# Halving the width of the output projection's matmuls in a fused attention and feed-forward kernel

## The chip, the cores and the metric

The kernel runs on one core of a Trainium2 chip. A core has a matrix engine (TensorE, "PE" in the profile, whose weight loads are listed apart as "PEld"), a vector engine (VectorE, "DVE"), a scalar engine (ScalarE, "ACT"), a general engine (GpSimd, "POOL") and a queue engine (SyncE, "SP"), and 16 DMA engines. Matmuls read SBUF and write PSUM. The metric is the device time in microseconds; lower is better.

A matmul has a stationary operand (up to 128 x 128, put into the array by a weight load) and a moving operand (128 rows, up to 512 columns, streamed through it). The result has as many columns as the moving operand.

## The reference

For each of 8 batches, with u and v of 3008 x 256 and z of 3008 x 64, and then for all 24064 rows together:

```
scores = (z @ z.T) / 3008
attn   = max(scores, 0) ** 2
x      = u * (attn @ v)              # 24064 x 256
h      = x @ w_in                    # 256 -> 2048
g      = h * cos(h)
out    = g @ w_out                   # 2048 -> 256, float32
```

The last product is what the change concerns; the text calls it y.

## The kernel before, in words

Rows are worked on in slots of 512: six per batch, the last of 448, so NSLOT = 48 slots. The feed-forward part has 48 blocks too: those with index 5 modulo 12 have 384 rows (`mwidth`), and the 64 rows that they leave over are put into the last block of the next batch (tile xodd), so that all others have 512. Operands are 16-bit floats, sums are fp32 in PSUM.

A slot has two phases. Phase A (`phase_a`) computes attention: score matmuls (line 187, two 64-row matmuls at a time), ReLU on ACT (line 200), the square on DVE (lines 205 and 208), and value matmuls with v as stationary operand (line 254), summed in the PSUM tiles M and E. DVE and ACT join the two partial sums (lines 266, 267) and multiply by u (line 282), which gives x, with the model width on partitions.

Phase B (`phase_b`) computes the feed-forward part in an order that is written out by hand:

```
seq_b = "h0 y0 h1 y1 h2 y2 h3 y3 h4 y4 h5 y5 y6 y7 st h6 h7".split()
```

An h step (`emit_h`, line 396) makes 256 of the 2048 inner columns: four matmuls of 512 columns into an E tile, with w_in blocks as stationary operand, then cos by a sine on ACT (line 404) and h * cos(h) on DVE (line 406) into a tile g with the inner width on partitions. A y step (`emit_y`, line 426) takes one such g tile of two inner blocks `ft`: for each, and for each of the up to four 128-row blocks `k`, `y_block` issues one matmul (line 418) whose stationary operand is the 128 x 128 block of g and whose moving operand is the 256 columns of w_out16 for that ft. The sums of the four row blocks lie in the two M banks, two per bank (`y_bank`), over all 16 ft; the first matmul of a bank starts its sum, the last stops it. The step `st` (`store_y`) copies M to SBUF on ACT (line 437) and sends it out from SP's queue (line 448). The steps h0 to h3 of the order above belong to the same block as its y steps, and are the block's last four; h4 to h7 are the first four of the next block, whose y steps come one phase B later. There are 47 phases B. The last block goes through `last_y`, which does the row blocks 0 and 1 beside the last h steps and then 2 and 3 one after the other, block 3 in an E bank.

At the start, z of the first batch is turned on the PE: `turn_on_pe` (line 517) issues 24 matmuls in transpose mode, each with a new 128 x 128 block of z as stationary operand and 128 columns of an identity as moving operand. Some matmuls on a tile of zeros (lines 532 and 556) stand around them.

The program order on each engine is the order in which the kernel text emits (`manual_schedule`); nothing moves instructions between engines or in time. Transposes of attention pieces (line 240) and of u (line 156), and stores, go through SP's queue; loads go through POOL's.

Of the kernel before, what the change touches and what calls it, by code (L numbers as in the profile page):

```python
# [14 lines left out]
def kernel(  # L15
# [9 lines left out]
    nc = tc.nc  # L25
# [6 lines left out]
    P = 128  # L32
# [5 lines left out]
    NFT = Dff // P  # L38
# [26 lines left out]
    w_out16 = kpool.tile([P, NFT, D], FP16, name="w_out16")  # L65
# [38 lines left out]
    z16s, zTs, vs, u16s, uTs, xs, gs = {}, {}, {}, {}, {}, {}, {}  # L104
# [281 lines left out]
    def mwidth(m):  # L386
        return 3 * P if m % (2 * NC) == NC - 1 else CW
# [23 lines left out]
    def y_bank(m, k):  # L411
        if m == NSLOT - 1 and k == 3:
            return E[0][:, 0, 0:D]
        return M[k // 2][:, (k % 2) * D:(k % 2 + 1) * D]

    def y_block(m, ft, k):
        final = m == NSLOT - 1
        nc.tensor.matmul(  # L418
            y_bank(m, k),
            gs[m, ft // 2][:, ft % 2, k * P:(k + 1) * P],  # L420
            w_out16[:, ft, :],
            start=(ft == 0 and (k % 2 == 0 or (final and k == 3))),
            stop=(ft == NFT - 1 and (k % 2 == 1 or k == mwidth(m) // P - 1 or (final and k == 2))),
        )

    def emit_y(m, i):
        for ft in range(2 * i, 2 * i + 2):
            for k in range(mwidth(m) // P):
                y_block(m, ft, k)

    def store_y(m):
        nblk = mwidth(m) // P
# [19 lines left out]
    def last_y(m):  # L452
        b, J = m // NC, m % NC
        for i in range(4):
            emit_h(m, 4 + i)
            for ft in range(2 * i, 2 * i + 2):
                y_block(m, ft, 0)
                y_block(m, ft, 1)
        for ft in range(8, NFT):
            y_block(m, ft, 0)  # L460
            y_block(m, ft, 1)
        for k in range(4):
            if k >= 2:
                for ft in range(NFT):
                    y_block(m, ft, k)
            o = opool.tile([P, 2, D], FP32, name="o")
            nc.scalar.activation(
                o[:, 0, :], y_bank(m, k),
                AF.Copy, bias=0.0, scale=inv_s2,
            )  # L470
            t0 = b * S + J * CW + k * P
            if k < 3:
                nc.sync.dma_start(out[t0:t0 + P, :], o[:, 0, :])
            else:
                nc.sync.dma_start(out[t0:t0 + H, :], o[0:H, 0, :])
                nc.scalar.dma_start(out[b * S - H:b * S, :], o[H:P, 0, :])
# [3 lines left out]
    def phase_b(s):  # L480
        for c in seq_b:
            i = int(c[1]) if c[1].isdigit() else 0
            if c == "st":
                store_y(s - 2)
            elif c[0] == "y":
                emit_y(s - 2, i)
            elif i < 4:
                emit_h(s - 2, 4 + i)
            elif s - 1 < NSLOT:
                emit_h(s - 1, i - 4)  # L490
            if c in ("h1", "h3", "h5"):
                emit_turns((0, 0), 1)
# [154 lines left out]
```

## Time and profile before

| | |
|---|---|
| median of 8 runs | 1231.68 us (1228.88 to 1235.65) |
| profiled execution | 1229.59 us |
| its span, first to last instruction | 1227.8 us |
| mean granted PE clock | 0.999 of full speed |
| PE busy | 99%, 9775 matmuls and 9775 weight loads |
| DVE busy / ACT busy | 65% / 66% |
| y matmuls (line 418) | 3008, mean 273 ns from start to modelled end |
| y weight loads (line 418) | 3008, mean 98 ns |

The profile comes from one execution. Matmuls are pipelined: one starts before the former has ended, so the mean duration of one is longer than the distance between starts, and only the latter adds up along the PE. In the tables of groups, the first number after the bar is the time in which at least one instruction of the group was busy, then comes the mean of one; after the second bar stands how long the engine sat idle just before them, and what ended that. In rows in order of time, the first number is the start, the second is how long the stretch lasted, both in microseconds, and "xN" is the number of instructions.

### The profile page before, as it was taken

Reading aid. Unit: us, or ns where it says so; the run is one execution under the profiler, and the core shown is the slowest. Engines: PE = TensorE matmul, PEld = TensorE weight load, DVE = VectorE, ACT = ScalarE, POOL = GpSimd, SP = SyncE. Lnnn points to the kernel's source line nnn. Section 1 sums busy time; section 2 is a strip of 40 time slices with the busy share of each in tenths; the row PEclk is TensorE's granted clock in tenths of the full one; section 3 lists DMA queues with packets and bytes.
Section 4 is the critical chain, followed back from the end, with each engine's and each line's share of the span. In section 5 each row is a group of like instructions: output and inputs, shape, how many; then the busy total and the mean of one; then the engine's idle time right before and its main releaser. Section 6 shows DMA issues by size and latency. Waiting matters only on the chain.

```text
span 1227.8 us, 23274 instructions
## 1 busy us (share of the span) xinstructions
PE 1217.6 (99%) x9775; PEld 694.9 (57%) x9775; DVE 803.0 (65%) x943; ACT 810.4 (66%) x923; POOL 131.3 (11%) x184
## 2 busy tenths in 40 slices
PE   8999999999999999999999999999999999999998
PEld 4455555555555556555555555655555555555565
DVE  6856666666666666666666666666666666666555
ACT  7856666667666666667666676666666666666445
POOL 3120300003000030000310002100211001000000
PEclk9999999999999999999999999999999999999999
DMA  9998998349773499725977359763697637953201
GB/s 155 182 172 153 138 158 142 63 98 165 140 126 74 89 153 165 120 70 100 172 129 123 71 102 165 145 125 65 115 178 123 114 73 106 157 103 70 47 18 52
DMA packets 467162, 144.80 MB, mean 118 GB/s; under 512 B 391537, under 2 KB 466801, under 8 KB 467057
## 3 DMA queue, kind: packets, MB, share of 16 engines
q1 hardware_dynamic: 368304, 110.11, 50.2%
q0 software_dynamic: 97216, 32.78, 28.3%
q8 instruction: 76, 1.25, 0.4%
q10 hardware_dynamic: 1536, 0.43, 0.2%
q14 instruction: 30, 0.24, 0.1%
HBM read 66.32 MB, written 24.64 MB: 74 GB/s over the span
## 4 chain that ended last, share of the span: by engine, by line
PE 94%; DMA 2%; issue 2%; ACT 1%; DVE 1%; POOL 0%; ACTq 0%; DVEq 0%; POOLq 0%
PE M L418 26%; PE E L396 26%; PE M L254 19%; PE E L254 18%; PE E L187 5%; DMA u<-in_u_dram 1%; ACT r L200 1%; DMA uT<-u 1%; PE E L532 0%; DVE g L406 0%; ACT c L404 0%; DVE A L208 0%; DVE s L267 0%; PE E L418 0%; DVE A L205 0%
## 5 line engine op out<-in xcount | busy, mean ns | idle before, releaser
L406 DVE SCALAR_TENSOR_TENSOR g<-E,c 128x1024 f16<-128x1024 f32 (+1 forms) x384 | 456.3, 1201 | 218.2 <-ACT c L404 217.0
L404 ACT ACTIVATE c<-E 128x1024 f16<-128x1024 f32 (+1 forms) x384 | 380.9, 1006 | 183.0 <-PE E L396 182.6
L200 ACT ACTIVATE r<-E 128x512 f16<-128x512 f32 (+1 forms) x342 | 327.9, 967 | 112.2 <-PE E L187 106.9
L418 PE MATMUL M<-w_out,g 128*128 128x256 f16 x2992 | 373.7, 273 | 1.0 <-DVE g L406 0.6
L254 PEld LDWEIGHTS <-v 64*128 64x128 f16 x4512 | 217.7, 94 | 259.7 <-issue 19.8
L396 PE MATMUL E<-x,w_in 128*128 128x512 f16 (+1 forms) x1408 | 347.4, 374 | 1.4 <-DVE g L406 0.7
L418 PEld LDWEIGHTS <-g 128*128 128x128 f16 x3008 | 294.2, 98 | 94.0 <-DVE g L406 0.9
L254 PE MATMUL M<-A,v 64*128 64x512 f16 (+1 forms) x2256 | 282.6, 372 | 0.3 <-DVE s L267 0.3
L254 PE MATMUL E<-A,v 64*128 64x512 f16 (+1 forms) x2256 | 277.5, 372 | 0.0
L205 DVE TENSOR_TENSOR A<-r 128x1024 f16<-128x1024 f16 x240 | 165.5, 692 | 103.9 <-ACT r L200 102.9
L396 PEld LDWEIGHTS <-w_in 128*128 128x128 f16 x1536 | 146.4, 98 | 127.2 <-issue 21.7
L187 PE MATMUL E<-zT 64*128 64x512 f16 (+2 forms) x684 | 125.2, 361 | 2.3 <-DVE zT L527 1.1
L437 ACT ACTIVATE o<-M 128x512 f32<-128x512 f32 x94 | 50.2, 585 | 63.4 <-PE M L418 63.4
L136 POOL DMA_DIRECT2D u<-in_u_dram x48 | 36.8, 770 | 461.5 <-DMA uT<-u 460.5
L208 DVE TENSOR_TENSOR A<-r 128x512 f16<-128x512 f16 (+1 forms) x102 | 57.7, 567 | 41.6 <-ACT r L200 40.6
L136 POOL DMA_DIRECT2D v<-in_v_dram x48 | 35.9, 754 | 401.8 <-PE E L187 338.7
L282 DVE TENSOR_TENSOR x<-s,uT 128x512 f16<-128x512 f32 (+1 forms) x88 | 59.5, 679 | 8.3 <-DMA uT<-u 5.5
L187 PEld LDWEIGHTS <-zT 64*128 64x128 f16 x684 | 34.6, 94 | 43.1 <-issue 4.3
L267 DVE TENSOR_TENSOR s<-E,s 128x512 f32<-128x512 f32 (+1 forms) x48 | 32.6, 680 | 34.1 <-ACT s L266 34.1
L266 ACT COPY s<-E 128x512 f32<-128x512 f32 (+1 forms) x48 | 27.7, 578 | 39.7 <-PE E L254 39.7
L267 DVE TENSOR_TENSOR s<-M,s 128x512 f32<-128x512 f32 (+1 forms) x48 | 32.3, 674 | 6.0 <-ACT s L266 6.0
L266 ACT COPY s<-M 128x512 f32<-128x512 f32 (+1 forms) x48 | 27.5, 573 | 8.2 <-PE M L254 7.8
(34 smaller groups left out, 118.2 us busy)
## 6 DMA issues: line engine op xcount, KB each, us to landing
out_dram<-o SPq DMA_DIRECT2D x87, 256.0 KB, 2.6
v<-in_v_dram POOLq DMA_DIRECT2D x40, 256.0 KB, 6.8
u<-in_u_dram POOLq DMA_DIRECT2D x40, 256.0 KB, 9.1
z<-in_z_dram POOLq DMA_DIRECT2D x14, 368.0 KB, 15.1
A<-A SPq DMA_TRANSPOSE x207, 4.4
v<-in_v_dram POOLq DMA_DIRECT2D x8, 192.0 KB, 10.9
u<-in_u_dram POOLq DMA_DIRECT2D x8, 192.0 KB, 4.4
out_dram<-o SPq DMA_DIRECT2D x10, 128.0 KB, 2.7
```

The costliest lines, as they stand in the source:

```text
L136: nc.gpsimd.dma_start(t[:, 0:full, :], src[b, g * CW:g * CW + full * P, :].rearrange("(j p) d -> p j d", p=P),)
L187: nc.tensor.matmul(e[:, t, 0:W], zT[t * H:(t + 1) * H, k * P:(k + 1) * P], zT[t * H:(t + 1) * H, J * CW:J * CW + W], start=True, stop=True,)
L200: nc.scalar.activation(r[:, :, 0:W], e[:, :, 0:W], AF.Relu)
L205: nc.vector.tensor_tensor(a4, r4, r4, ALU.mult)
L208: nc.vector.tensor_tensor(a4, r[:, :, 0:W], r[:, :, 0:W], ALU.mult)
L254: nc.tensor.matmul(bank[:, 0:width(J)], vs[b, k // 4][t * H:(t + 1) * H, k % 4, dh * P:(dh + 1) * P], value_rhs(b, J, k, t), start=start, ...
L267: nc.vector.tensor_tensor(s1[:, 0:W], b1[:, 0:W], s0[:, 0:W], ALU.add)
L282: nc.vector.tensor_tensor(x[:, dh, 0:nk * P].rearrange("p (k j) -> p k j", j=P), s1[:, 0:nk * P].rearrange("p (k j) -> p k j", j=P), uT[:, ...
L396: nc.tensor.matmul(e[:, f, 0:W], w_in16[:, k, ft * P:(ft + 1) * P], x[:, k, 0:W], start=(k == 0), stop=(k == 1),)
L404: nc.scalar.activation(c[:, :, 0:W], e[:, :, 0:W], AF.Sin, bias=half_pi, scale=inv_s2)
L406: nc.vector.scalar_tensor_tensor(g[:, :, 0:W], e[:, :, 0:W], 1.0, c[:, :, 0:W], ALU.mult, ALU.mult)
L418: nc.tensor.matmul(y_bank(m, k), gs[m, ft // 2][:, ft % 2, k * P:(k + 1) * P], w_out16[:, ft, :], start=(ft == 0 and (k % 2 == 0 or (final ...
```

## The change

Each y matmul of 256 columns becomes two of 128 columns, one for each half `q` of the output width. In `emit_y` the half is a loop around the row blocks k, so that for each ft four matmuls with four different g blocks write the first half, and then four with the same four g blocks write the second; every matmul has a weight load of another block than the one before it. In `last_y`, which calls `y_block` without a half, the two halves of a row block follow each other. The start flag stands on half 0 of the first matmul of a bank, the stop flag on half 1 of the last.

```diff
-    def y_block(m, ft, k):
+    def y_block(m, ft, k, d=None):
         final = m == NSLOT - 1
-        nc.tensor.matmul(
-            y_bank(m, k),
-            gs[m, ft // 2][:, ft % 2, k * P:(k + 1) * P],
-            w_out16[:, ft, :],
-            start=(ft == 0 and (k % 2 == 0 or (final and k == 3))),
-            stop=(ft == NFT - 1 and (k % 2 == 1 or k == mwidth(m) // P - 1 or (final and k == 2))),
-        )
+        for q in range(2) if d is None else (d,):
+            nc.tensor.matmul(
+                y_bank(m, k)[:, q * P:(q + 1) * P],
+                gs[m, ft // 2][:, ft % 2, k * P:(k + 1) * P],
+                w_out16[:, ft, q * P:(q + 1) * P],
+                start=(ft == 0 and q == 0 and (k % 2 == 0 or (final and k == 3))),
+                stop=(ft == NFT - 1 and q == 1 and (k % 2 == 1 or k == mwidth(m) // P - 1 or (final and k == 2))),
+            )
 
     def emit_y(m, i):
         for ft in range(2 * i, 2 * i + 2):
-            for k in range(mwidth(m) // P):
-                y_block(m, ft, k)
+            for q in range(2):
+                for k in range(mwidth(m) // P):
+                    y_block(m, ft, k, q)
```

## The prediction

> **What bounds the kernel now.** I read the page's shares first, then the waits, then the chain, and last the order of time in one phase B and in the first microseconds.
>
> ```profile
> span 1227.8 us, 23274 instructions
> PE 1217.6 (99%) x9775; PEld 694.9 (57%) x9775; DVE 803.0 (65%) x943; ACT 810.4 (66%) x923; POOL 131.3 (11%) x184
> PE 94%; DMA 2%; issue 2%; ACT 1%; DVE 1%; POOL 0%; ACTq 0%; DVEq 0%; POOLq 0%
> ```
>
> PE is busy 99% of the span and carries 94% of the chain that ended last. A busy PE row alone proves little, because matmul records overlap and their ends are modelled. The idle columns decide:
>
> ```profile
> L418 PE MATMUL M<-w_out,g 128*128 128x256 f16 x2992 | 373.7, 273 | 1.0 <-DVE g L406 0.6 <-DVE s L267 0.4
> L396 PE MATMUL E<-x,w_in 128*128 128x512 f16 x1280 | 322.0, 379 | 1.4 <-DVE g L406 0.7 <-DVE s L267 0.7
> L418 PEld LDWEIGHTS <-g 128*128 128x128 f16 x3008 | 294.2, 98 | 94.0 <-DVE g L406 0.9 <-issue 0.6
> ```
>
> All y matmuls together (L418: 2992 into M, 16 into E) waited 1.0 us in the whole run, and those of h (L396) 1.4 us. So whatever one y matmul costs more is paid in full. The 273 ns of one is start to modelled end; what counts is the distance between starts, and that is read from the chain, where a stretch ends at the start of the next:
>
> ```profile
> 118.05 2.62 PE M L418 x24
> ```
>
> 24 matmuls in 2.62 us: 109.2 ns for one of 256 columns. In the same place, h of 512 columns takes 0.86 us for four (117.18 to 118.05), about 216 ns each. A halving of the columns from 512 to 256 thus saves not quite half: 2 x 109.2 - 216 = 2.4 ns are paid per matmul, however many columns it has.
>
> The changed kernel's new form, 128 columns with a fresh 128x128 stationary block every time, is already in this trace: the transposes of z at the start (L517; stationary z16, moving id16).
>
> ```profile
> 5.85 0.40 PE L517 MATMUL turned<-id,z 128*128 128x128 f16 x4
> 6.08 0.39 PE L517 MATMUL turned_e<-id,z 128*128 128x128 f16 x4
> 6.30 0.59 PE L556 MATMUL M<-warm 128*128 128x512 f16 x2
> 5.84 0.45 PEld L517 LDWEIGHTS <-z 128*128 128x128 f16 x8 [0.42 <-DVE zT L527]
> ```
>
> The first three rows are the matmuls, the fourth is the weight loads of the eight transposes. The second four take from 6.08 to 6.30: 0.22 us, 55 ns each. All eight, with the first that has no load ahead of it, take 0.45 us: 56 ns each. Eight loads fit into the same 0.45 us although each is listed with 98 ns, so loads overlap one another and a load is not a limit at 98 ns. These are transposes and write 16-bit results, where y accumulates in fp32; that they stream at the same rate is my assumption, supported by the 2.4 ns that both have above half of the next size.
>
> **What the Trainium skill says.** "TensorE: Matmul & The Clock Gate", section "Wait — 56ns, not 53.3ns?", gives start-to-start as N ÷ 2.4 GHz plus about 2.5 ns: 55.6 ns at 128 columns and 215.7 at 512. The trace agrees: 55 to 56, 109.2 and 216. The same page, section "Step-by-step: what each phase is for", says that the loads of the next block run while the present matmul streams, through a read port of their own; the eight overlapped loads agree. But its section "Back-to-back issue gap" gives, for a sustained stream of load and matmul pairs, about 81 ns at 128 columns and 131 at 512. The 512 figure is contradicted here (216), and no run of 128 columns longer than eight is in this trace, so 81 stays as a rival.
>
> **The change part by part.**
>
> Removed: 3008 matmuls of 256 columns with 3008 loads. On the path: 3008 x 109.2 ns = 328.5 us.
>
> Added: 6016 matmuls of 128 columns with 6016 loads. Columns streamed and products are the same. The price of one lies between 55 ns (second four transposes) and 56.3 ns (all eight, including the uncovered first). The rule from the halving, 109.2/2 + 1.2 = 55.8 ns, lies between them, and I take it. The cost is 2 x 55.8 - 109.2 = 2.4 ns per old matmul: 3008 x 2.4 = 7.2 us. With 55 ns it would be 0.8 x 3008 = 2.4 us, with 56.3 ns 3.4 x 3008 = 10.2 us. The low end needs a fixed cost that shrinks with the matmul, and the rounding of 0.22 us to 0.01 allows 54 to 56, so I lean up: 7.5 us.
>
> The second load of each g block: 3008 more loads, hidden behind the previous matmul, cost nothing while a load needs less than the 55.8 ns of that matmul. The eight transposes show that it fits. If that cover were gone and loads went at their listed 98 ns end to end, a pair would be 196 ns and the kernel 3008 x 87 = 261 us slower; the eight loads in 0.45 us exclude that.
>
> Moved: within one ft, emit_y now goes over the four k for columns 0 to 127 and then again for 128 to 255. The same accumulator address is hit again after 8 x 55.8 = 446 ns instead of 4 x 109.2 = 437; in last_y's one-k loops after 112 instead of 109. Nothing shorter, so no new hazard; I set zero. The M banks still alternate every two matmuls as k goes 0, 1, 2, 3. The last y of a block still closes both halves, so store_y's copy (L437) starts when the PE gets there; it had 63.4 us of waiting for L418 and is behind no one.
>
> Waits and DMAs: none is added. The first y of each g tile waits for DVE's g as before. Behind PE nothing is late that isn't late by the same 0.16 us per slot (7.5 us over 47 slots); ACT at 66% and DVE at 65% have room, so they follow. Instruction fetch: 19550 PE instructions become 25566. In a slot, 64 y matmuls and 32 of h take 7.0 + 6.9 = 13.9 us for 192 instructions, 72 ns each; afterwards 320 instructions in 14.1 us, 44 ns each, and 28 ns each inside a run of y. Phase A's pairs run two loads and two matmuls per 216 ns, 54 ns per instruction, the densest sustained rate that this trace shows. So the supply is shown for 54, and for 28 only in a burst of eight pairs that may have been queued up. Zero if the queue refills quickly; if 54 were its limit, 320 x 54 = 17.3 us per slot instead of 14.1, which is 3.2 x 47 = 150 us. I take zero: no idle time of PE is put down to issue in a dense stretch.
>
> Sum: +7.5 us on the profiled execution, 1229.59 us with its span of 1227.8, gives 1237.1 with a span of 1235.3. The profiled execution is 2.1 us under the median of the runs, 1231.68; against that the forecast is 1239.2.
>
> **The rivals.**
>
> (a) Sustained pairs don't keep up: either instruction supply at 54 ns (1231.7 + 150 = 1382) or the page's 81 ns per pair ((162 - 109.2) x 3008 = 159 us, 1391). For it: no long run of this form is in the trace, and the 24 matmuls of y5 to y7 in each slot become 48 on end. Against it: the eight transposes, and 24 y at a steady 109.2.
>
> (b) A small extra per load, such as 58 to 65 ns per matmul because a load just misses its cover now and then while DMA and the other engines read SBUF: 7 to 21 ns per old matmul, 20 to 62 us, 1252 to 1294. For it: the transposes ran at 6 us, when ACT, DVE and the transfers were less dense than later. Against it: they had no sign of jitter.
>
> (c) Not slower: PE waits in phase B swallow the extra. The mechanism is that h(i+1) waits for an E buffer which DVE's g frees at a fixed time, so that longer y fills the wait. It decides from 5 us of such idle time, which would leave less than 2.5 us, 0.2%. The profile has 1.0 + 1.4 us before L418 and L396 in all, so at most 2.4 of 7.5 us can go this way: 1236.7. To end at 1232 it would also need the fixed cost at its low end of 0.8 ns.
>
> (d) The change doesn't do what it says: equal stationary blocks could be loaded once. Then only last_y, where the two halves of a k follow each other, could skip loads, and hidden loads save nothing; the filler (L556) repeats one block and has a load for each of its four matmuls. 1239.2 all the same.
>
> **How the numbers follow.** The fixed cost per matmul, (d) included: 0.84, with 1235 to 1243 as its own range (2.4 to 10.2 us from the price's bounds). Rival (b) 0.08, (a) 0.04, (c) 0.04. About 0.2%, 2.5 us, is what a measurement of this kernel can tell from no change; 7.5 us is three times that. Faster has only half of (c)'s bad luck and no mechanism of its own: 0.01; same 0.04, from (c) and the low price; slower 0.95. The range takes the likeliest case and, above it, 4 us towards (b), which is also what the median of a set of runs may stand off by (the runs before spread from 1228.88 to 1235.65): 1235 to 1247.
>
> **What would show it.** L418 with 6016 matmuls of 128 columns and as many loads; 24 old matmuls of y5 to y7 become 48, taking about 2.68 us in the chain instead of 2.62; idle before L418 and L396 still about 1 us; h and phase A unchanged at 216 ns. A run of 48 that takes 3 us or more, or gaps put down to issue before L418's loads, would prove me wrong towards (b) or (a); a span that grows by under 2.5 us, with L418's starts at 54.6 ns, would prove the fixed cost wrong.

## The result and the profile after

The changed kernel takes 1239.35 us (median of 11 runs, 1237.70 to 1244.06) against 1231.04 us for the kernel before (32 runs, 1228.84 to 1236.64): a ratio of 1.0066, with a 95% interval of 1.0053 to 1.0079. It is 8.3 us slower; the interval allows 6.5 to 9.7 us. The forecast was 1239.2 us.

The page of the changed kernel, its first lines and the chain by engine:

```profile
span 1238.5 us, 29290 instructions
PE 1225.8 (99%) x12783; PEld 736.9 (60%) x12783; DVE 802.8 (65%) x943; ACT 806.5 (65%) x923; POOL 131.2 (11%) x184
PE 93%; DMA 2%; issue 2%; ACT 1%; DVE 1%; POOL 0%; SPq 0%; ACTq 0%; DVEq 0%; POOLq 0%
```

PE has 3008 matmuls and 3008 loads more, and every other engine has as many instructions as before, with the same busy time to within 4 us. PE is still busy 99% of the span and still carries the chain.

The groups by form (busy, mean of one, idle before, in us and ns):

```profile
L419 PE MATMUL M<-w_out,g 128*128 128x128 f16 x5984 | 381.1, 219 | 1.1 <-DVE g L406 0.6 <-DVE s L267 0.5
L396 PE MATMUL E<-x,w_in 128*128 128x512 f16 x1280 | 322.0, 379 | 2.8 <-DVE s L267 2.1 <-DVE g L406 0.7
L254 PE MATMUL M<-A,v 64*128 64x512 f16 x1880 | 240.7, 376 | 1.5 <-DMA A<-A 1.2 <-DVE s L267 0.3
L419 PEld LDWEIGHTS <-g 128*128 128x128 f16 x6016 | 360.0, 98 | 66.3 <-DVE g L406 0.8 <-issue 0.6
```

The y matmuls (now line 419) waited 1.1 us in all, where they had waited 1.0 before. A load is still listed with 98 ns, but 6016 of them are busy for only 360.0 us, which is 60 ns each: they overlap one another.

The chain in one phase B of the changed kernel (start, length, engine and line):

```profile
624.26 0.89 PE M L419 x16
625.15 0.86 PE E L396 x4
626.02 2.68 PE M L419 x48
```

48 matmuls of 128 columns take 2.68 us, 55.8 ns each. h is untouched: four in 0.86 us, as in the row of the kernel before from which the prediction took its 216 ns:

```profile
117.18 0.86 PE E L396 x4
```

In the whole run the price is therefore 2 x 55.8 - 109.2 = 2.4 ns for each of 3008 old matmuls, 7.2 us. That one phase B speaks for all can be seen by adding up the distances from every y start to the next start on PE, less the early wait described next: 330.3 us in each of the three profiles of the kernel before, 337.9 and 337.6 us in the two of the changed one, 7.3 to 7.6 us more.

The two profiled spans differ by 10.7 us, 3.5 us more than 7.2. The rows of h and of the value matmuls hold 2.6 us of it: h waited 2.1 us for DVE's s, once, near 86 us, where the kernel before had waited 0.7, and the value matmuls waited 1.2 us for the turned pieces A where they had not waited at all. The other 0.9 us is not assigned. Whether these waits belong to the change is asked in the last three runs.

### The profile page after: what moved, and what is told of

Read it like the earlier page. It is cut to its first block, busy times and chain, and to the rows that moved or that the text cites. A ratio compares the mean times of both kernels' runs of the same rounds, so it can differ in the third digit from the quotient of the medians.

```text
span 1238.5 us, 29290 instructions
## 1 busy us (share of the span) xinstructions
PE 1225.8 (99%) x12783; PEld 736.9 (60%) x12783; DVE 802.8 (65%) x943; ACT 806.5 (65%) x923; POOL 131.2 (11%) x184
## 4 chain that ended last, share of the span: by engine, by line
PE 93%; DMA 2%; issue 2%; ACT 1%; DVE 1%; POOL 0%; SPq 0%; ACTq 0%; DVEq 0%; POOLq 0%
PE M L419 26%; PE E L396 25%; PE M L254 19%; PE E L254 18%; PE E L187 5%; DMA u<-in_u_dram 2%; ACT r L200 1%; DMA uT<-u 0%; DVE g L406 0%; DMA A<-A 0%; PE E L534 0%; ACT c L404 0%; DVE A L208 0%; DVE s L267 0%; PE E L419 0%
## 5 line engine op out<-in xcount | busy, mean ns | idle before, releaser
L419 PEld LDWEIGHTS <-g 128*128 128x128 f16 x6016 | 360.0, 98 | 66.3 <-DVE g L406 0.8
L419 PE MATMUL M<-w_out,g 128*128 128x128 f16 x5984 | 381.1, 219 | 1.1 <-DVE g L406 0.6
L396 PEld LDWEIGHTS <-w_in 128*128 128x128 f16 x1536 | 134.6, 98 | 122.1 <-issue 23.1
L267 DVE TENSOR_TENSOR s<-M,s 128x512 f32<-128x512 f32 (+1 forms) x48 | 32.3, 674 | 6.0 <-ACT s L266 6.0
```

The lines of the kernel that those rows point to most:

```text
L267: nc.vector.tensor_tensor(s1[:, 0:W], b1[:, 0:W], s0[:, 0:W], ALU.add)
L396: nc.tensor.matmul(e[:, f, 0:W], w_in16[:, k, ft * P:(ft + 1) * P], x[:, k, 0:W], start=(k == 0), stop=(k == 1),)
L419: nc.tensor.matmul(y_bank(m, k)[:, q * P:(q + 1) * P], gs[m, ft // 2][:, ft % 2, k * P:(k + 1) * P], w_out16[:, ft, q * P:(q + 1) * P], st ...
```

## The experiments

The theory: each matmul costs its columns and about 2.4 ns, whatever it multiplies, and weight loads are hidden. The rivals: the cost is that of a new stationary block; or the load has a price of its own that a 128-column matmul happens to cover; or the supply of instructions sets a limit. Each ratio below is against runs of the kernel before on the same chip.

### The same block twice

```diff
         for ft in range(2 * i, 2 * i + 2):
-            for q in range(2):
-                for k in range(mwidth(m) // P):
-                    y_block(m, ft, k, q)
+            for k in range(mwidth(m) // P):
+                y_block(m, ft, k)
```

> The changed kernel with the halves innermost: the two 128-column matmuls of one g block follow each other, so that every second load brings the block that is already there. Theory (each matmul pays about 2.4 ns beside its columns, loads are hidden): nothing changes, about 1239 us, y starts 55.8 ns apart. Rival (the cost comes from a new stationary block at every matmul): half of the 8 us goes, about 1235 us, or all of it, 1231 us.

Measured: 1239.77 us (1236.73 to 1241.87), ratio 1.0065 (1.0045 to 1.0084). A line of its page, and its chain:

```profile
PE 1225.5 (99%) x12783; PEld 736.9 (59%) x12783; DVE 803.4 (65%) x943; ACT 810.5 (65%) x923; POOL 131.1 (11%) x184
...
625.22 0.86 PE E L396 x4
626.08 2.68 PE M L419 x48
```

The same 2.68 us for 48. All 12783 loads are still there: a block that is already in place is loaded again, and that load is as well hidden as one of a new block. So it costs nothing that the block is a new one each time, and the first rival falls.

### 192 and 64 columns

```diff
+        cut = (0, 192, D)
         for q in range(2) if d is None else (d,):
             nc.tensor.matmul(
-                y_bank(m, k)[:, q * P:(q + 1) * P],
+                y_bank(m, k)[:, cut[q]:cut[q + 1]],
                 gs[m, ft // 2][:, ft % 2, k * P:(k + 1) * P],
-                w_out16[:, ft, q * P:(q + 1) * P],
+                w_out16[:, ft, cut[q]:cut[q + 1]],
```

> The changed kernel with the output width cut into 192 and 64 columns instead of 128 and 128: the same number of matmuls, loads and columns. Theory: only the number of matmuls counts, about 1239 us. Rival (cover of the load): matmuls of 64 columns no longer cover the next load; with 55 ns per load 82.4 + 55.8 - 111.6 = 26.6 ns more per pair, 80 us, about 1319 us.

Measured: 1238.51 us (1237.50 to 1239.15), ratio 1.0055 (1.0036 to 1.0075). The chain of this kernel:

```profile
622.40 0.89 PE M L420 x16
623.29 0.86 PE E L396 x4
624.16 2.68 PE M L420 x48
```

Half the matmuls now have 64 columns and last only some 29 ns each (29.2 in the run with quarters below), and the run of 48 still takes 2.68 us. The load is not just covered at 128 columns; it has room. Down to 64 columns, with the same columns streamed in all, what counts is how many matmuls there are.

### h in pieces of 128 columns, y as before

From the kernel before:

```diff
             for k in range(2):
-                nc.tensor.matmul(
-                    e[:, f, 0:W],
-                    w_in16[:, k, ft * P:(ft + 1) * P],
-                    x[:, k, 0:W],
-                    start=(k == 0),
-                    stop=(k == 1),
-                )
+                for c0 in range(0, W, P):
+                    nc.tensor.matmul(
+                        e[:, f, c0:c0 + P],
+                        w_in16[:, k, ft * P:(ft + 1) * P],
+                        x[:, k, c0:c0 + P],
+                        start=(k == 0 and c0 == 0),
+                        stop=(k == 1 and c0 + P == W),
+                    )
```

> The kernel before, with y as it was, and each h matmul cut into pieces of 128 columns of x with the same w_in block: 1408 matmuls become four and 128 become three, 4480 more. Theory: 4480 x 2.4 = 10.8 us, about 1242 us. Rival (the cost belongs to y, to its g blocks or its accumulators): 1231 us.

Measured: 1241.90 us (1240.14 to 1247.49), ratio 1.0092 (1.0069 to 1.0115), which is 11.5 us over the 1230.40 us of the kernel before on the same chip, where 10.8 were expected. The chain of this kernel:

```profile
624.10 0.89 PE E L397 x16
624.99 0.87 PE M L419 x8
625.86 0.89 PE E L397 x16
626.75 2.62 PE M L419 x24
```

Sixteen pieces of h take 0.89 us, as sixteen halves of y do, where four whole ones took 0.86; y is back at 2.62 us for 24. So the fixed cost comes with a matmul wherever it stands, and belongs neither to y nor to its g blocks or accumulators. One thing stays open here and in all runs: each matmul has a weight load of its own (on every page PE and PEld have the same count), so whether the 2.4 ns are the matmul's or are what its load leaves uncovered isn't told apart.

### Quarters of 64 columns

```diff
-        for q in range(2) if d is None else (d,):
+        for q in range(4) if d is None else (d,):
             nc.tensor.matmul(
-                y_bank(m, k)[:, q * P:(q + 1) * P],
+                y_bank(m, k)[:, q * (D // 4):(q + 1) * (D // 4)],
                 gs[m, ft // 2][:, ft % 2, k * P:(k + 1) * P],
-                w_out16[:, ft, q * P:(q + 1) * P],
+                w_out16[:, ft, q * (D // 4):(q + 1) * (D // 4)],
```

with the loop in `emit_y` and the stop flag set to four pieces as well.

> The changed kernel with four quarters of 64 columns, again a new g block at every matmul: 12032 y matmuls and loads. Theory: 26.7 + 2.4 = 29.1 ns apart, 4 x 29.1 - 109.2 = 7.2 ns per old matmul, 3008 x 7.2 = 22 us, about 1253 us. Rival (a load needs about the 55 ns that a 128-column matmul happens to cover): 4 x 55.8 - 109.2 = 114 ns, 343 us, about 1574 us. A load that needs 40 ns would give 1384 us. Supply of instructions at 54 ns each as the limit would give far above 1600 us.

Measured: 1262.69 us (1258.23 to 1265.15), ratio 1.0249 (1.0224 to 1.0275): 32.3 us slower, where the theory said 22. Two places of this kernel's chain:

```profile
611.99 0.23 PE M L419 x8
612.22 0.58 issue
612.80 2.73 PE M L419 x88
...
638.97 2.80 PE M L419 x96
```

and its two groups by form that waited for issue:

```profile
L419 PE MATMUL M<-w_out,g 128*128 128x64 f16 x11968 | 397.7, 193 | 3.9 <-issue 2.9 <-DVE g L406 0.5 <-DVE s L267 0.4
L396 PE MATMUL E<-x,w_in 128*128 128x512 f16 x1280 | 323.3, 380 | 5.5 <-DVE s L267 3.9 <-issue 0.8 <-DVE g L406 0.7
```

A clean run takes 2.80 us for 96, 29.2 ns each: that term of the theory stands, 7.2 to 7.6 ns per old matmul or 22 to 23 us, and a load fits in 29 ns too. What the theory left out: now and then PE has nothing to run although no wait that the profile lists holds it, as from 612.22 on. These gaps come to 2.9 + 0.8 = 3.7 us of idle time in this execution, and the early wait for DVE's s was 3.9 us instead of 0.7. With 23 us these make 30 of the 33.2 us by which the profiled spans differ. Of the last 3 us, 0.9 lies in the four h matmuls right after the early wait, which took 1.73 us instead of 0.86: from 90.9 to 94.2 us the granted clock was 0.50. The rest is not assigned.

The trace says what the gaps are. The pages list a DMA queue of the kind "instruction" (packets, MB, share of the 16 engines), here for the kernel before, the changed one, the quarters and the eighths:

```profile
q8 instruction: 76, 1.25, 0.4%
...
q8 instruction: 100, 1.64, 0.5%
...
q8 instruction: 147, 2.41, 0.8%
...
q8 instruction: 240, 3.93, 1.1%
```

Divided by the matmuls and loads of the run, this is 64 bytes per PE instruction in all four kernels, so the queue brings PE its instructions, 256 in a packet. Each of the six gaps ends 1.2 to 1.6 us after one of these packets has ended, and so does each of the 29 of at least 0.28 us in the next run, 1.2 to 1.7 us after; moments picked at random would fall so in 4% and 8% of cases. In the gaps PE waits for instructions that arrived late. Here they stand 152 to 155 us apart or twice that, at most one per batch of six slots, so density alone doesn't make them; why a packet comes late wasn't tested. The supply thus begins to show at 576 PE instructions per slot in 14.4 us, 25 ns each; it is far from the 54 ns that the prediction's first rival feared.

### Eighths of 32 columns

The same edit with eight pieces.

> The changed kernel with eight pieces of 32 columns, a new g block at every matmul: 24064 y matmuls and loads. Theory carried on (columns and about 2.4 ns each, loads hidden): 8 x (13.3 + 2.4) - 109.2 = 16.4 ns per old matmul, 49 us, about 1280 us. Rival (a load, or the issue of a load and a matmul, has a floor of its own; the Trainium skill, TensorE: Matmul & The Clock Gate, section Wait - 56ns, not 53.3ns?, states about 25 ns start to start): 8 x 25 - 109.2 = 91 ns, 273 us, about 1504 us. Rival (supply of instructions, which left gaps of 0.4 to 1.1 us in the run of quarters at some 25 ns per instruction): more gaps, at 20 ns for each of 1088 instructions in a slot 21.8 us instead of 13.9, 370 us, about 1600 us; the gaps are then put down to issue, and between them starts stay at 16 or 25 ns.

Measured: 1572.12 us (1569.25 and 1574.98), ratio 1.2774 (1.2711 to 1.2837): 341 us slower. Two lines of this kernel's chain, and its groups of y and h by form:

```profile
719.15 1.59 PE M L419 x64
...
721.61 4.79 PE M L419 x192
```

```profile
L419 PE MATMUL M<-w_out,g 128*128 128x32 f16 x23936 | 649.7, 177 | 51.3 <-issue 50.7 <-DMA w_out<-in_moe_w_out_dram 0.6
L396 PE MATMUL E<-x,w_in 128*128 128x512 f16 x1280 | 330.9, 387 | 0.8 <-DVE g L406 0.7
```

Here the theory breaks down: 192 in 4.79 us are 24.9 ns each, where columns and 2.4 ns would give 15.7. There is a floor of about 25 ns from start to start, which the Trainium skill states on the page "TensorE: Matmul & The Clock Gate", section "Wait — 56ns, not 53.3ns?", and this trace agrees at 32 columns, the only width below 64 that was run. It costs 8 x 24.9 - 109.2 = 90 ns per old matmul, 271 us; 50.7 us more are gaps put down to issue. Together they are 322 of the 339 us by which the spans differ. Of the rest, 8.9 us lie in h, which is unchanged and yet busy for 330.9 us where it had been 322.0. The granted clock was lower (0.982 in the mean, against 0.999), and where it falls h is slow: after a gap of 2.53 us from 745.73 on, the clock was 0.50 from 749.0 to 752.2 us, and the four h matmuls there took 1.42 us instead of 0.86. Whether load or matmul makes the floor isn't told apart: both come in pairs here.

### The two kernels once more

No edit: three more profiles of one execution each, to see whether the early wait and the wait for A belong to the change.

> The kernel before, unchanged, for another profile. The profiles so far differ by 10.7 us of span, of which the distance between y starts gives 7.3; the rest is a wait of h for DVE's s near 86 us (0.7 against 2.1 us) and value matmuls that waited for the turned pieces A (0 against 1.2 us). If these waits are scatter of the transfers, the kernel before shows them too at times, with the early wait between 0.7 and over 2 us; if the change causes them, it shows 0.7 and 0 again.

> The kernel before once more, as e6: a third profile of the same kernel, to see how far the early wait and the wait for A scatter without any change.

> The changed kernel, unchanged, for another profile. y starts again 55.8 ns apart, no gaps put down to issue in phase B. If the early wait near 86 us and the wait for A are scatter, they come out different from 2.1 and 1.2 us, and the span moves with them, 1235.5 to 1239; if they are of the change, both stand.

Measured, the kernel before: 1230.16 and 1230.79 us, spans 1228.4 and 1229.0. From their waits (total, times, longest), first the one, then the other:

```profile
PE E L396 <- DVE s L267: 0.9, 1, 0.9
```

```profile
PE E L396 <- DVE s L267: 0.9, 1, 0.9
...
PE M L254 <- DMA A<-A: 0.4, 1, 0.4
```

The changed kernel: 1237.52 us. Its first line, and from its waits:

```profile
span 1235.7 us, 29290 instructions
```

```profile
PE M L254 <- DMA A<-A: 0.9, 1, 0.9
```

The early wait for s, 2.1 us in the first profile of the changed kernel, is absent from the second, and the span is 2.8 us shorter. That wait scatters from one execution of the changed kernel to the next, so 2.1 us is not a steady cost of the change; in the other runs it was 2.3 (same block twice), 0.7 (192 and 64), 0.4 (h in pieces) and 3.9 us (quarters), and it is missing with eighths. The wait for A is less clear: 0, 0 and 0.4 us in three profiles of the kernel before, 1.2 and 0.9 in two of the changed one. Near 100 us the pieces come from transposes in SP's queue behind those of the next batch's z. The other traces bear on it: 1.4 us with the same block twice, 0.8 with 192 and 64, and 1.2 with h in pieces, whose y is the old one; but 0.4 with quarters and none with eighths. So all five profiles of kernels that are 7 to 12 us slower have 0.8 us or more, and no profile of the kernel before has. It doesn't need the new form of y and doesn't grow with the number of matmuls. It may come from the shift in time that the extra matmuls make, which isn't shown. If the change does add it, it is about 1 us, and it would bring 7.2 to the 8.3 that was measured.

## Why the prediction was right

- **What bounds the kernel.** That PE has no slack that could hide anything held: the y matmuls waited 1.0 us before and 1.1 after, and the fixed cost of 2.4 ns came out in full.
- **The price of the new form.** 55.8 ns, taken from the halving of 512 to 256 and bracketed by the eight transposes at the start, is what 48 in 2.68 us give, and that stretch was named to two decimals. It was the halving that fixed the price: the transposes alone, at 55 to 56.3 ns, left anything from 2.4 to 10.2 us. The assumption that matmuls in transpose mode stream at the rate of ordinary ones held as far as these can tell.
- **The second load at no cost.** Held, beyond whatever part of the 2.4 ns may be a load's, and with more room than was claimed: loads are hidden under 64-column matmuls (29.2 ns), and the same block twice changes nothing.
- **Zero for the order of the halves.** Held: the other order gives the same 2.68 us and, with 1239.77 us, the same time.
- **The sum.** 7.5 us were forecast against the median before; 8.3 (6.5 to 9.7) were measured. The profiles give 7.2 to 7.6 to the spacing of y starts. The first pair of profiles alone would have given 10.7, of which some 1.4 are the scatter of the early wait. That the forecast of 1239.2 us lies so close to 1239.35 is partly luck: it started from a median of 8 runs that was 0.6 us above that of 32, and its step was 0.8 us too small; the lean from 7.2 to 7.5 had no measurement behind it. The range that was given to the likeliest case, 1235 to 1243, is also about 1 us too high for its own bounds, which from 1231.7 give 1234.1 to 1241.9; the result lies in both.
- **Rival (a), pairs that don't keep up.** It fell: y's matmuls had no gap that is put down to issue, their loads one of 0.6 us, as in the kernel before, and starts 55.8 ns apart in runs of 48 leave no room for 81 ns per pair, the figure of the section "Back-to-back issue gap" on the Trainium skill's page "TensorE: Matmul & The Clock Gate". As to the supply of instructions, it was the right kind of danger at the wrong size: gaps put down to issue appear at 25 ns per instruction (3.7 us with quarters) and are large with eighths, 50.7 us.
- **Rival (b), now and then an uncovered load.** It fell: 16 and 48 matmuls come at 55.6 and 55.8 ns, in 0.89 and 2.68 us.
- **Rival (c), waits that swallow the extra.** It fell as argued: there was hardly any such idle time to fill, and y's did not shrink (1.0 us before, 1.1 after).
- **Rival (d).** 6016 loads are there; none is left out, and none either in the run where equal blocks follow each other throughout. What leaving one out would save was therefore not measured.
- **Idle before h.** "About 1 us" was wrong for the profiled execution, 2.8 us, of which 2.1 are the early wait; in the second profile that wait is absent and 0.9 us for DVE's g are left.

## What to carry to other kernels

When PE starts back to back with no idle time, the number of matmuls has a price of its own, here 2.4 ns each with its load, so of the widths tried the widest moving operand is best, and the stationary block may change each time at no measured cost. Read the distance between starts from the chain (length of a stretch over its count) and look for the new form elsewhere in the same trace: two wider forms gave the price of six thousand matmuls, and eight transposes bracketed it. With shorter matmuls other limits show: gaps in the supply of instructions at 64 columns, and at 32 larger ones and a floor of about 25 ns.

## What the runs showed of the hardware that was not expected

- Loads of 128 x 128 blocks that the profile lists with 98 ns can follow each other every 29.2 ns, and with their matmuls every 24.9 ns: the listed duration of a load doesn't say how often one can be done.
- A load of the block that was loaded last isn't left out (12783 loads in the run with the same block twice), and it costs no more or less than one of a new block: 2.68 us for 48 matmuls either way.
- With quarters and eighths, PE idles for 0.3 to 4.3 us at a time, put down to issue. All 35 such gaps end 1.2 to 1.7 us after a packet of the instruction queue has ended, so PE ran out of instructions. What made the packets late wasn't tested.
- Idle time of PE can cost more than itself: after waits of 3.9 us (quarters) and 2.53 us (eighths) the granted clock was 0.50 for some 3 us, and h took about twice its time while that lasted.
